# Token blocks of another size, operands in another place of the on-chip memory, and the fill of missing keys as a stage of its own

## The chip, the cores and the metric

The kernel runs on one core of one Trainium2 chip. The metric is the device time of one launch in microseconds: the median of 3 runs of the kernel before is 997.27 us (996.07 to 997.98). The core's engines work from queues of their own: TensorE (PE in the profile, with its weight loads as PEld), VectorE (DVE), ScalarE (ACT), GpSimd (POOL) and SyncE (SP), which issues most DMAs.

## The reference

Attention over chunks of 32 queries, each with 8 memory keys and up to 56 neighbouring keys, then two feed-forward stages over 3072 tokens, all in float32:

```python
for c in range(nc):                         # attention, 4 x 8 heads, 768 positions
    k_full = np.concatenate([mem_k, k[:, :, max(0, 32*c - 16):min(S, 32*c + 40)]], axis=2)
    v_full = ...                            # likewise
    a = softmax(0.125 * q_c @ k_full.T)
    out[:, :, 32*c:32*c + 32] = a @ v_full
x = out.transpose(0, 2, 1, 3).reshape(3072, 512)
x2 = ((x @ w_a) * (x @ w_b)) @ w_out        # w_a, w_b: 512 x 1536, w_out: 1536 x 512
h = x2 @ w_in                               # 512 x 1024
u = h * softmax(h)
y = ((u - mean(u)) / sqrt(var(u) + 1e-6) * g_ln) @ w_out2     # 1024 x 512
```

## The kernel before

Every product of the feed-forward stages is made of three matmuls (`mm3`, lines 376 to 378): operands are split into a high part and a rest, and high x rest, rest x high and high x high are added up in PSUM.

**Stage one** (`ab`, `gate`, `x2_step`) goes over blocks of tokens (`block_list`): 512, 256 and six times 384. In a block it goes over 12 slices f of the inner width 1536. One step f is 24 matmuls into `pab` (a and b, 12 each, over 4 slices of the model width), the gate (VectorE multiplies a and b at L393, ScalarE rounds to `gh` at L396, VectorE takes the rest `gl` at L400), and 12 matmuls into four `acc` banks (`x2_step`), which run one step later than their gate. The weights (`w`, 12 slots of 12 KB a partition) are the stationary operand; x (`xh`, `xl`) and the gate results (`gh`, `gl`) are streamed, one column a token. So a step is 36 matmuls as wide as the block. At a block's end `x2_out` writes the result to DRAM (`x2d`).

**Attention** works on quads of 4 chunks (128 tokens, 24 quads), for the block that comes next, in the slots between the matmuls of the current one: three slots a step, 36 a block. Its stages are `att_S` (fill of missing keys where a sequence begins or ends, L143 and L145, then 64 small matmuls for the scores), `att_M` (maximum), `att_X` (exponential, L174), `att_N` (normalisation, from L182), `att_T` (transposes), `att_V` (products, L219, and the copy to `xh`) and `att_L` (the rest `xl`, L242). Scores, transposed weights and products of all quads share one PSUM tile, `at`. The table in the main loop gives each stage its slot: quads are spread evenly over the slots, and for block 0 the slots are written out. The loads of q, k and v have two buffers, so a load waits for the products of the quad two before it.

**Block 0** also converts the weights of stage one (`w1_abs` to `w1_lo`: ScalarE and VectorE on 128 x 1536 pieces), and **the last block** those of stage two (`w2_*`) into slots 0 to 5.

**Stage two** goes over 24 tiles of 128 tokens: 24 matmuls of 512 columns for h (`h_mm`), softmax and normalisation, 8 transposes, 24 matmuls of 512 columns for the output (`o_mm`; the last two tiles in halves of 256). Here the converted weights are streamed and the tokens are stationary.

**Order.** In the attention at the start, block 0 and the last block the order of TensorE, VectorE and ScalarE is the program's. In the blocks between only TensorE's is; a planner orders the rest.

**Memory.** Pools lie one behind the other in the order in which they are opened: constants, `wp` (weight slots 0 to 5, 72 KB a partition), `wq` (slots 6 to 11, 72 KB), loads, attention tiles and conversion tiles (some 38 KB), then `xp` (x of two blocks, 28 KB) and `gp` (10 KB). All from `wq` on is given back after stage one, and stage two's tiles lie from the start of `wq`.

Of the kernel before, what the change touches and what calls it, by code (L numbers as in the profile page):

```python
# [8 lines left out]
F32 = mybir.dt.float32  # L9
# [9 lines left out]
P = 128  # L19
B, H, S, D = 4, 8, 768, 64  # L20
NMEM = 8
CQ = 32
CK = 64
NCH = 4
GQ = NCH * CQ
# [3 lines left out]
NG = S // GQ  # L29
NP = H // 2  # L30
# [4 lines left out]
NF2 = DFF2 // P  # L35
# [5 lines left out]
NEG = -3.0e38  # L41
# [6 lines left out]

def block_list():

    sizes = [512, 256] + [384] * 6
    out, t = [], 0
    for n in sizes:
        out.append((t, n))
        t += n
    assert t == NTOK
    return out
# [3 lines left out]
def fused_kernel(  # L61
# [9 lines left out]
    nc = tc.nc  # L71
# [3 lines left out]

    const = ctx.enter_context(tc.tile_pool(name="const", bufs=1))
    dram = ctx.enter_context(tc.tile_pool(name="dram", bufs=1, space=bass.MemoryType.DRAM))
    wp = ctx.enter_context(tc.tile_pool(name="wp", bufs=1))

    ident = const.tile([P, P], F32, name="ident")  # L80
    gln_sb = const.tile([P, NF2], F32, name="gln_sb")
    mhalf = const.tile([P, 1], F32, name="mhalf")

    x2d = [dram.tile([P, NP, n], F32, name=f"x2d{i}") for i, (_, n) in enumerate(blocks)]

    work = ExitStack()
    wq = work.enter_context(tc.tile_pool(name="wq", bufs=1))
    ld_p = work.enter_context(tc.tile_pool(name="ld", bufs=2))
# [1 line left out]
    at_p = work.enter_context(tc.tile_pool(name="atp", bufs=2))  # L90
    z_p = work.enter_context(tc.tile_pool(name="zp", bufs=2))
    sm_p = work.enter_context(tc.tile_pool(name="sm", bufs=3))
    x_p = work.enter_context(tc.tile_pool(name="xp", bufs=1))
    g_p = work.enter_context(tc.tile_pool(name="gp", bufs=2))
    ps_at = work.enter_context(tc.tile_pool(name="ps_at", bufs=1, space=PSUM))
    ps_ab = work.enter_context(tc.tile_pool(name="ps_ab", bufs=1, space=PSUM))
    ps_acc = work.enter_context(tc.tile_pool(name="ps_acc", bufs=4, space=PSUM))
# [2 lines left out]
    quads = {}  # L100
# [10 lines left out]
    def slot_tile(i, shape, dtype, name):  # L111

        return (wp if i < NS2 else wq).tile(shape, dtype, tag=f"w{i}", name=name)

    def att_load(qi, slot=None):


        n = NP * (GQ + GK) + NCH * NP * D
        if slot is None:
            t = ld_p.tile([P, n], F32, tag="qkv", name="qkv")  # L120
        else:
            t = slot_tile(slot, [P, n], F32, "qkv")
        q, k = NP * GQ, NP * (GQ + GK)
        if slot is None:
            nc.sync.dma_start(t, qkv[qi])
        else:
            nc.sync.dma_start(t[:, 0:k], qkv[qi, :, 0:k])
        quads[qi] = dict(
            q=t[:, 0:q].rearrange("d (p t) -> d p t", p=NP),
            k=t[:, q:k].rearrange("d (p t) -> d p t", p=NP),  # L130
            v=t[:, k:n].rearrange("k (c p d) -> k c p d", c=NCH, p=NP),
        )
        return lambda: nc.sync.dma_start(t[:, k:n], qkv[qi, :, k:n])

    def att_S(qi):


        st = quads[qi]
        g = qi % NG
        full = ps_at.tile([P, 2, 512], F32, tag="at", name="s")  # L140
        s = full[:, :, 0:NP * CK].rearrange("q r (p k) -> q r p k", p=NP)
        if g == 0:
            nc.vector.memset(s[0:CQ, :, :, 0:16], NEG)  # L143
        if g == NG - 1:
            nc.vector.memset(s[GQ - CQ:GQ, :, :, 56:64], NEG)  # L145
        for p in range(NP):
            for c in range(NCH):
                lo = 16 if (g == 0 and c == 0) else 0
                hi = 56 if (g == NG - 1 and c == NCH - 1) else CK
                k0 = (c // 2) * KW + (c % 2) * CQ  # L150
                for r in range(2):
                    rows = slice(64 * r, 64 * r + 64)
                    nc.tensor.matmul(
                        s[CQ * c:CQ * c + CQ, r, p, lo:hi],
                        st["q"][rows, p, CQ * c:CQ * c + CQ],
                        st["k"][rows, p, k0 + lo:k0 + hi],
                        start=True,
                        stop=True,
                    )
        st["s"] = s  # L160

    def att_M(qi):
        s = quads[qi]["s"]
# [6 lines left out]
    def att_X(qi):  # L170
        st = quads[qi]
        s = st.pop("s")
        e = a_p.tile([P, NP, 2, CK], F32, tag="E", name="E")
        nc.scalar.activation(  # L174
            out=e.rearrange("q p r k -> q r p k"), in_=s, func=AF.Exp, scale=SCALE
        )
        st["e"] = e.rearrange("q p r k -> q (p r) k")
# [80 lines left out]
    def w_range(z):  # L258

        zi = z.bitcast(I32)  # L260
        nc.vector.tensor_scalar(out=z, in0=z, scalar1=W_LO, scalar2=W_HI, op0=ALU.max, op1=ALU.min)
        nc.vector.tensor_scalar(
            out=zi, in0=zi, scalar1=3, scalar2=0x3FFFFFF8,
            op0=ALU.logical_shift_left, op1=ALU.bitwise_and,
        )
# [43 lines left out]
    def w1_range(f, part=None):  # L309
        cols = slice(0, NS * WC) if part is None else slice(part * WC, (part + 1) * WC)  # L310
        w_range(zs[f][0][:, cols])
# [235 lines left out]
    def N(i):  # L547
        att_N(i, nc.vector)
# [7 lines left out]

    w1_abs(0, 0)
    w1_range(0, 0)
    att_S(0)
    att_M(0)  # L560
    w1_abs(0, 1)
    att_X(0)
    w1_range(0, 1)
    att_S(1)
    N(0)
    w1_abs(0, 2)
# [1 line left out]
    att_M(1)  # L568
    w1_range(0, 2)
    att_X(1)  # L570
    att_S(2)
    w1_sign(0)
    w1_low(0)
# [3 lines left out]
    att_M(2)  # L577
    att_L(0)
    att_X(2)
    att_S(3)  # L580
    w1_add(0)
    w1_hi(0)
# [34 lines left out]
    for bi in range(NB):  # L617
        qs = slots_for(bi)
        nslots = 3 * NF1
        plan = {}  # L620
        if qs:
            stages = (att_S, att_M, att_X, att_N, att_T, att_V, att_L)
            per = (nslots - 6) / len(qs)
            for j, qi in enumerate(qs):
                b0 = int(j * per)
                at = [b0 + k for k in (0, 0, 0, 0, 4, 5, 5)]
                if bi == 0:

                    at = ((27, 28, 28, 29, 31, 32, 33), (30, 30, 30, 31, 33, 34, 35))[j]
                for k, fn in zip(at, stages):  # L630
                    plan.setdefault(k, []).append((fn, qi))
            att_load(qs[0])
            if bi == 0:
                att_load(qs[1])
        loaded = 1 if bi else 2
        slot = 0

        def run_slot():
            nonlocal slot, loaded
            for fn, qi in plan.get(slot, []):  # L640
                fn(qi)
                if fn is att_V and loaded < len(qs):
                    att_load(qs[loaded])
                    loaded += 1
            slot += 1

        for f in range(NF1):
            if (bi, f) == (1, 0):

                in_order.close()  # L650
                in_order.enter_context(tc.manual_schedule(engines={ENG.PE}))
            if (bi, f) == (NB - 1, 0):
                in_order.close()
                in_order.enter_context(
                    tc.manual_schedule(engines={ENG.PE, ENG.DVE, ENG.Activation})
                )

            c0, c1 = (f - 4, f - 3) if bi == NB - 1 else (-1, -1)
            n = blocks[bi][1]
            pa = ab(bi, f, 0)  # L660
            a_sb = g_p.tile([P, n], F32, tag="asb", bufs=1, name="asb", padded_shape=[P, NMAX])
            nc.scalar.copy(a_sb, pa)  # L662
            run_slot()
            pb = ab(bi, f, 1)
            if bi == 0 and f + 3 < NF1:
                w1_abs(f + 3)
            if 0 <= c1 < NS2:
                w2_abs(c1)
            gh, gl = gate(bi, a_sb, pb)
            if bi == 0 and f + 2 < NF1:  # L670
                w1_add(f + 2)
                w1_hi(f + 2)
            if 0 <= c0 < NS2:
                w2_add(c0)
                w1_hi(c0)
            gate_lo(a_sb, gh, gl)
            if bi == 0 and f + 3 < NF1:
                w1_low(f + 3)
                w1_range(f + 3)
            if bi == 0 and f + 2 < NF1:  # L680
                w1_lo(f + 2)
            if bi == 0 and f + 3 < NF1:
                w1_sign(f + 3)
            if 0 <= c1 < NS2:
                w1_low(c1)
                w_range(zs[c1][0])
            if 0 <= c0 < NS2:
                w2_lo(c0)
            if 0 <= c1 < NS2:
                w1_sign(c1)  # L690
            run_slot()
            if pend is not None:
                x2_step(*pend)
                if pend[1] == NF1 - 1:
                    x2_out(pend[0])
            pend = (bi, f, gh, gl)
            run_slot()
            if bi == 0 and f == NF1 - 1:
                x2_step(*pend)
                x2_out(0)  # L700
                pend = None
            if bi == NB - 1 and 1 <= f <= NS2:

                w2_load(f - 1)
# [117 lines left out]
```

## Time and profile before

| | |
|---|---|
| median of 3 runs | 997.27 us (996.07 to 997.98) |
| profiled execution, its time | 996.04 us |
| its span, first to last instruction | 994.3 us |
| mean granted clock of TensorE | 0.998 of full speed |
| busy: PE, DVE, ACT, POOL | 963.1, 480.0, 305.5, 38.0 us |
| attention at the start and block 0 | to 147.4 us |
| blocks 1 to 7 | 147.4 to 703.1 us |
| stage two | from 704.0 us |

Times in the rows are microseconds from the start of the span, unless they are marked ns. Matmuls are pipelined: the duration of one runs from its start to its end and overlaps the next, so what a matmul costs is the distance from start to start. A tile name like `pab<-xh,w` is what an instruction writes and reads, and L376 is a line of the kernel. What stands in brackets at a row's end is idle time of the engine before it and what ended it. The granted clock is the share of the full 2.4 GHz that TensorE was given.

### The profile page before, as it was taken

What the parts mean: (1) busy time and instruction counts of PE and PEld (TensorE: products, weight loads), DVE (VectorE), ACT (ScalarE), POOL (GpSimd) and SP (SyncE); (2) the same over time, 40 slices, a digit from 0 to 9 for tenths busy, and PEclk for the clock granted to TensorE, in tenths of its full rate; (3) what the DMA queues carried; (4) which work ended last, traced back from release to release, by engine and by line L of the source; (5) the groups of instructions that cost most, each with busy time, mean ns of one, the idle gap of its engine ahead of it and who ended that gap; (6) DMA issues with size and microseconds to landing.
All of it is one profiled execution on the core that took longest, in us unless ns stands there. A gap on an engine that the chain in (4) does not pass through costs nothing.

```text
span 994.3 us, 18094 instructions
## 1 busy us (share of the span) xinstructions
PE 963.1 (97%) x8016; PEld 878.0 (88%) x8016; DVE 480.0 (48%) x783; ACT 305.5 (31%) x464; POOL 38.0 (4%) x54
## 2 busy tenths in 40 slices
PE   4899899999999999999999999998999999999998
PEld 3688679999999999999999999998878888888887
DVE  6999933323223223322322322298575656665553
ACT  4777522222222212122222221364232332222222
POOL 0000000000000000000000000000000000000000
PEclk9999999999999999999999999999999999999999
DMA  9950032211101112111110100451211111111000
GB/s 374 423 251 1 1 117 72 97 61 57 49 32 49 49 49 80 49 48 61 68 49 31 51 1 1 162 209 33 84 43 43 44 43 53 43 43 40 25 22 33
DMA packets 27631, 75.62 MB, mean 76 GB/s; under 512 B 2016, under 2 KB 16864, under 8 KB 23584
## 3 DMA queue, kind: packets, MB, share of 16 engines
q1 hardware_dynamic: 27280, 73.67, 20.2%
q8 instruction: 63, 1.03, 0.5%
q0 software_dynamic: 272, 0.79, 0.3%
q14 instruction: 16, 0.13, 0.0%
HBM read 61.87 MB, written 12.58 MB: 75 GB/s over the span
## 4 chain that ended last, share of the span: by engine, by line
PE 84%; DVE 11%; issue 3%; DMA 1%; ACT 1%; SPq 0%; POOL 0%; DVEq 0%; ACTq 0%
PE pab L376 11%; PE pab L378 11%; PE pab L377 11%; PE acc L376 6%; PE acc L377 6%; PE acc L378 6%; PE psh L455 4%; PE pso L514 4%; PE pso L513 4%; PE pso L515 4%; PE psh L456 4%; PE psh L457 4%; PE px L219 3%; DVE z L277 3%; DVE z L269 2%
## 5 line engine op out<-in xcount | busy, mean ns | idle before, releaser
L376 PE MATMUL pab<-xh,w 128*128 128x384 f32 (+2 forms) x768 | 264.5, 344 | 3.2 <-ACT asb L662 2.2
L377 PE MATMUL pab<-xl,w 128*128 128x384 f32 (+2 forms) x768 | 259.3, 338 | 0.0
L378 PE MATMUL pab<-xh,w 128*128 128x384 f32 (+2 forms) x768 | 259.2, 337 | 0.0
L393 DVE TENSOR_TENSOR asb<-asb,pab 128x384 f32<-128x384 f32 (+2 forms) x96 | 53.1, 553 | 253.8 <-PE pab L378 253.8
L376 PEld LDWEIGHTS pab<-xh,w 128*128 128x128 f32 x768 | 144.9, 189 | 11.3 <-ACT asb L662 3.2
L377 PEld LDWEIGHTS pab<-xl,w 128*128 128x128 f32 x768 | 145.1, 189 | 4.5 <-DVE xl L242 0.2
L378 PEld LDWEIGHTS pab<-xh,w 128*128 128x128 f32 x768 | 144.9, 189 | 4.6
L377 PE MATMUL acc<-gl,w 128*128 128x384 f32 (+2 forms) x384 | 129.5, 337 | 1.9 <-DVE gl L400 1.8
L376 PE MATMUL acc<-gh,w 128*128 128x384 f32 (+2 forms) x384 | 131.2, 342 | 0.0
L378 PE MATMUL acc<-gh,w 128*128 128x384 f32 (+2 forms) x384 | 129.1, 336 | 0.0
L662 ACT COPY asb<-pab 128x384 f32<-128x384 f32 (+2 forms) x96 | 45.8, 477 | 179.9 <-PE pab L378 179.2
L396 ACT CAST gh<-asb 128x384 fp32r<-128x384 f32 (+2 forms) x96 | 49.3, 514 | 159.3 <-DVE asb L393 159.3
L514 PE MATMUL pso<-w,ll 128*128 128x512 f32 (+1 forms) x208 | 79.5, 383 | 0.6 <-DVE ll L502 0.6
L513 PE MATMUL pso<-w,lh 128*128 128x512 f32 (+1 forms) x208 | 77.9, 375 | 1.5 <-ACT lh L501 1.5
L515 PE MATMUL pso<-w,lh 128*128 128x512 f32 (+1 forms) x208 | 77.7, 374 | 0.0
L377 PEld LDWEIGHTS acc<-gl,w 128*128 128x128 f32 x384 | 72.1, 188 | 5.0 <-DVE gl L400 2.9
L455 PE MATMUL psh<-w,x2hl 128*128 128x512 f32 x192 | 75.0, 390 | 0.6 <-ACT x2hl L437 0.6
L457 PE MATMUL psh<-w,x2hl 128*128 128x512 f32 x192 | 74.9, 390 | 0.0
L456 PE MATMUL psh<-w,x2hl 128*128 128x512 f32 x192 | 74.8, 390 | 0.0
L376 PEld LDWEIGHTS acc<-gh,w 128*128 128x128 f32 x384 | 72.1, 188 | 2.9
L400 DVE TENSOR_TENSOR gl<-asb,gh 128x384 fp32r<-128x384 f32 (+2 forms) x96 | 53.4, 557 | 42.9 <-ACT gh L396 42.9
L378 PEld LDWEIGHTS acc<-gh,w 128*128 128x128 f32 x384 | 72.1, 188 | 2.2
(67 smaller groups left out, 1056.4 us busy)
## 6 DMA issues: line engine op xcount, KB each, us to landing
qkv<-qkv_dram SPq DMA_DIRECT2D x20, 1152.0 KB, 5.6
raw<-w1d_dram SPq DMA_DIRECT2D x11, 1536.0 KB, 24.8
out_dram<-ot SPq DMA_DIRECT2D x22, 256.0 KB, 2.0
x2r<-x2d SPq DMA_DIRECT2D x21, 256.0 KB, 3.1
x2d<-x2s SPq DMA_DIRECT2D x12, 384.0 KB, 2.5
raw<-win_dram SPq DMA_DIRECT2D x8, 512.0 KB, 5.4
raw<-wout_dram SPq DMA_DIRECT2D x8, 512.0 KB, 5.0
qkv<-qkv_dram SPq DMA_DIRECT2D x4, 640.0 KB, 9.1
```

Source lines behind the costliest of these rows:

```text
L376: nc.tensor.matmul(ps, wl, xh, start=first, stop=False)
L377: nc.tensor.matmul(ps, wh, xl, start=False, stop=False)
L378: nc.tensor.matmul(ps, wh, xh, start=False, stop=last)
L393: nc.vector.tensor_tensor(out=a_sb, in0=a_sb, in1=pb, op=ALU.mult)
L396: nc.scalar.copy(gh, a_sb)
L400: nc.vector.tensor_tensor(out=gl, in0=a_sb, in1=gh.bitcast(F32), op=ALU.subtract)
L455: nc.tensor.matmul(ps[:, hf], a, w[:, 1], start=(k == 0), stop=False)
L456: nc.tensor.matmul(ps[:, hf], b, w[:, 0], start=False, stop=False)
L457: nc.tensor.matmul(ps[:, hf], a, w[:, 0], start=False, stop=(k == NP - 1))
L513: nc.tensor.matmul(po, s["lh"][:, f], wl, start=(f == 0), stop=False)
L514: nc.tensor.matmul(po, s["ll"][:, f], wh, start=False, stop=False)
L515: nc.tensor.matmul(po, s["lh"][:, f], wh, start=False, stop=(f == NF2 - 1))
```

## The change

The block sizes become 512, 256, 512, 384, 512, 384, 512: seven blocks instead of eight. The pools `xp` and `gp` are opened directly behind the constants, ahead of `wp`, and are no longer given back before stage two; two small constants are padded, so that `xp` begins 3072 bytes into a partition (2176 bytes of it lie ahead of the kernel's own constants). The fill of missing keys leaves `att_S` and becomes the stage `att_P`, with a slot of its own: in the middle blocks the slot of `att_S`, in block 0 slot 29 for the second quad, ahead of the first quad's normalisation there (the list of slot 29 is reversed), while `att_T` and `att_V` of block 0 go one slot later.

```diff
-    sizes = [512, 256] + [384] * 6
+    sizes = [512, 256, 512, 384, 512, 384, 512]
...
+    ident = const.tile([P, P], F32, name="ident")
+
+    gln_sb = const.tile([P, NF2], F32, name="gln_sb", padded_shape=[P, 64])
+    mhalf = const.tile([P, 1], F32, name="mhalf", padded_shape=[P, 32])
+
+    x2d = [dram.tile([P, NP, n], F32, name=f"x2d{i}") for i, (_, n) in enumerate(blocks)]
+
+
+    x_p = ctx.enter_context(tc.tile_pool(name="xp", bufs=1))
+    g_p = ctx.enter_context(tc.tile_pool(name="gp", bufs=2))
     wp = ctx.enter_context(tc.tile_pool(name="wp", bufs=1))
...
-    x_p = work.enter_context(tc.tile_pool(name="xp", bufs=1))
-    g_p = work.enter_context(tc.tile_pool(name="gp", bufs=2))
...
+    def att_P(qi):
+        full = ps_at.tile([P, 2, 512], F32, tag="at", name="s")
+        s = full[:, :, 0:NP * CK].rearrange("q r (p k) -> q r p k", p=NP)
+        if qi % NG == 0:
+            nc.vector.memset(s[0:CQ, :, :, 0:16], NEG)
+        if qi % NG == NG - 1:
+            nc.vector.memset(s[GQ - CQ:GQ, :, :, 56:64], NEG)
+        quads[qi]["s"] = s
+
     def att_S(qi):
...
-        full = ps_at.tile([P, 2, 512], F32, tag="at", name="s")
-        s = full[:, :, 0:NP * CK].rearrange("q r (p k) -> q r p k", p=NP)
-        if g == 0:
-            nc.vector.memset(s[0:CQ, :, :, 0:16], NEG)
-        if g == NG - 1:
-            nc.vector.memset(s[GQ - CQ:GQ, :, :, 56:64], NEG)
+        s = st["s"]
...
+    att_P(0)
     att_S(0)
...
-            stages = (att_S, att_M, att_X, att_N, att_T, att_V, att_L)
+            stages = (att_P, att_S, att_M, att_X, att_N, att_T, att_V, att_L)
             per = (nslots - 6) / len(qs)
             for j, qi in enumerate(qs):
                 b0 = int(j * per)
-                at = [b0 + k for k in (0, 0, 0, 0, 4, 5, 5)]
+                at = [b0 + k for k in (0, 0, 0, 0, 0, 4, 5, 5)]
                 if bi == 0:
 
-                    at = ((27, 28, 28, 29, 31, 32, 33), (30, 30, 30, 31, 33, 34, 35))[j]
+                    at = ((27, 27, 28, 28, 29, 32, 33, 33), (29, 30, 30, 30, 31, 34, 35, 35))[j]
                 for k, fn in zip(at, stages):
                     plan.setdefault(k, []).append((fn, qi))
+            if bi == 0:
+
+                plan[29].reverse()
```

`att_P` also stands ahead of each of the other three `att_S` of the attention at the start.

## Rows read from the trace of the kernel before

**Rows 1.** The page: busy us (share) and count; granted clock in 40 slices, tenths.

```profile
PE 963.1 (97%) x8016; PEld 878.0 (88%) x8016; DVE 480.0 (48%) x783; ACT 305.5 (31%) x464; POOL 38.0 (4%) x54
...
PEclk9999999999999999999999999999999999999999
```

**Rows 2.** Timeline of TensorE, block 0: start us, us, instruction; six steps lie between.

```profile
58.38 0.40 PE L376 MATMUL pab<-xh,w 128*128 128x512 f32 x1
...
108.78 0.40 PE L376 MATMUL pab<-xh,w 128*128 128x512 f32 x1
```

**Rows 3.** Timeline of TensorE, block 3 (384 columns), two steps apart.

```profile
352.16 0.33 PE L376 MATMUL pab<-xh,w 128*128 128x384 f32 x1
...
364.64 0.33 PE L376 MATMUL pab<-xh,w 128*128 128x384 f32 x1
```

**Rows 4.** Timeline of TensorE, block 1 (256 columns), one step apart.

```profile
196.90 0.28 PE L376 MATMUL pab<-xh,w 128*128 128x256 f32 x1
...
201.14 0.28 PE L376 MATMUL pab<-xh,w 128*128 128x256 f32 x1
```

**Rows 5.** Timeline of TensorE, stage two: 44 matmuls apart, then 22 (256 columns).

```profile
819.92 0.39 PE L513 MATMUL pso<-w,lh 128*128 128x512 f32 x1
...
829.90 0.39 PE L515 MATMUL pso<-w,lh 128*128 128x512 f32 x1
...
987.91 0.28 PE L514 MATMUL pso<-w,ll 128*128 128x256 f32 x1
...
990.55 0.28 PE L515 MATMUL pso<-w,lh 128*128 128x256 f32 x1
```

**Rows 6.** Windows, block 3 and the last: us, busy of PE to POOL, clock, DMA, GB/s.

```profile
287.92:370.88 82.96, 82.96 (x830) 80.97 (x830) 23.16 (x44) 17.87 (x35) 3.13 (x3) 1.00 0.15 54
...
619.77:703.06 83.29, 79.24 (x445) 76.84 (x444) 54.40 (x65) 37.60 (x46) 2.29 (x3) 1.00 0.36 121
```

**Rows 7.** Timeline of VectorE, last block: four gates in turn.

```profile
656.97 0.55 DVE L393 TENSOR_TENSOR asb<-asb,pab 128x384 f32<-128x384 f32 x1
...
664.77 0.55 DVE L393 TENSOR_TENSOR asb<-asb,pab 128x384 f32<-128x384 f32 x1
...
673.10 0.55 DVE L393 TENSOR_TENSOR asb<-asb,pab 128x384 f32<-128x384 f32 x1
...
682.21 0.55 DVE L393 TENSOR_TENSOR asb<-asb,pab 128x384 f32<-128x384 f32 x1
```

**Rows 8.** Timeline of TensorE, last block: the starts of two steps in turn.

```profile
671.01 0.45 PE L376 MATMUL pab<-xh,w 128*128 128x384 f32 x1 [0.80 <-ACT asb L662]
...
680.13 0.45 PE L376 MATMUL pab<-xh,w 128*128 128x384 f32 x1 [0.78 <-ACT asb L662]
```

**Rows 9.** Timeline of all engines, block 0, up to the scores of quad 5.

```profile
122.78 0.60 ACT L174 ACTIVATE E<-s 128x512 f32<-128x512 f32 x1 [3.22 <-DVE s L166]
...
123.41 0.69 DVE L182 TENSOR_REDUCE sm<-E 128x8 f32<-128x512 f32 x1 [0.72 <-ACT E L174]
...
124.63 0.11 DVE L145 MEMSET s<- 32x64 f32 x1
...
124.84 0.89 PE L153 MATMUL s<-qkv 64*32 64x64 f32 x64 [3.71 <-ACT asb L662]
```

**Rows 10.** Timeline of VectorE, block 0: the gates of the steps f = 1 and 9.

```profile
51.02 0.68 DVE L393 TENSOR_TENSOR asb<-asb,pab 128x512 f32<-128x512 f32 x1
...
115.64 0.69 DVE L393 TENSOR_TENSOR asb<-asb,pab 128x512 f32<-128x512 f32 x1
```

**Rows 11.** Windows, the end of block 0: columns as in rows 6.

```profile
121.00:130.00 9.00, 5.29 (x77) 4.14 (x77) 4.22 (x9) 1.67 (x3) 1.04 (x1) 0.81 0.01 2
```

**Rows 12.** Timeline of all engines, block 1: products of its first quad, and their rest.

```profile
156.54 1.14 PE L219 MATMUL px<-AT,qkv 64*64 64x32 f32 x64
...
158.37 0.69 DVE L242 TENSOR_TENSOR xl<-px,xh 128x512 fp32r<-128x512 f32 x1 [2.74 <-ACT xh L237]
```

**Rows 13.** The page, DMA issues: count, KB each, median us from issue to landing.

```profile
qkv<-qkv_dram SPq DMA_DIRECT2D x20, 1152.0 KB, 5.6
```

More of the change, by code (lines that the diff above doesn't have):

```diff
@@ L77, in fused_kernel @@
     dram = ctx.enter_context(tc.tile_pool(name="dram", bufs=1, space=bass.MemoryType.DRAM))
+    ident = const.tile([P, P], F32, name="ident")
[4 more added lines that the diff above has]
+    g_p = ctx.enter_context(tc.tile_pool(name="gp", bufs=2))
     wp = ctx.enter_context(tc.tile_pool(name="wp", bufs=1))
[L80 to L84, printed above, removed]
     work = ExitStack()
@@ L159, in att_S @@
                     )
-        st["s"] = s
     def att_M(qi):
@@ L563, in fused_kernel @@
     w1_range(0, 1)
+    att_P(1)
     att_S(1)
@@ L570, in fused_kernel @@
     att_X(1)
+    att_P(2)
     att_S(2)
@@ L579, in fused_kernel @@
     att_X(2)
+    att_P(3)
     att_S(3)
```

## The prediction

> **What bounds the kernel now.** I read the page first: TensorE is busy for 97% of the span [rows 1], so the question is what one matmul costs. Busy time cannot say it, because matmuls overlap; the timeline can, from start to start over whole steps with no attention work in them. In block 0 six steps of 36 matmuls of 512 columns run from 58.38 to 108.78 us: 233.3 ns each [rows 2]. At 384 columns two steps run from 352.16 to 364.64: 173.3 ns [rows 3]. At 256 columns one step runs from 196.90 to 201.14: 117.8 ns [rows 4]. Stage two has 512 columns as well, and there 44 matmuls run from 819.92 to 829.90: 226.8 ns; its 256-column ones take 120.0 ns (22 from 987.91 to 990.55) [rows 5].
>
> At 2.4 GHz, the clock granted in all these stretches, 512, 384 and 256 columns take 213.3, 160.0 and 106.7 ns. What stands above that is 13.5 ns (512) and 13.3 ns (256) in stage two, and 20.0, 13.3 and 11.1 ns (512, 384, 256) in stage one. So only the 512-column matmul of stage one is dear. Its operands differ from stage two's in place: by the pools' sizes x, gh and gl lie behind 144 KB of weights and 38 KB of working tiles, from about 182 KB of a partition on, while stage two streams weights that lie in the lowest 75 KB. The weights' own place doesn't show: the steps of rows 2 take theirs from slots up to 75 KB apart, at one rate.
>
> Then the stages where TensorE waits. The windows give 82.96 us for a block of 384, busy throughout, and for the last block, which has no attention work beside it, 83.29 with 79.24 busy [rows 6]. In the last block VectorE converts stage two's weights, and it is the bound: its gates (L393) start 7.8, 8.3 and 9.1 us apart [rows 7], and TensorE's step beginning at 671.01 lasts 9.12 us where 36 x 173.3 ns = 6.24 are work [rows 8]. Last, the end of block 0: TensorE stops for 3.7 us before the scores of quad 5 (124.84) [rows 9]; the row names a copy of ScalarE (L662), but the scores also need the fill (L145), and that ends last, at 124.74.
>
> **The change part by part.** All sums are against the profiled execution, 996.04 us with a span of 994.27; the median of the runs is 997.27, 1.2 higher.
>
> *Block sizes.* Each block has 12 steps of 36 matmuls, 432. Behind block 0, before: 432 x (0.1178 + 6 x 0.1733) = 500.2 us. After, at the old price of 512 columns: 432 x (0.1178 + 3 x 0.2333 + 2 x 0.1733) = 503.0, so +2.9 us. Wider blocks alone lose.
>
> *x and the gate results in the lowest memory.* The trace has no stage-one matmul with its operands there. Nearest rows: stage two's 226.8 at 512 and 120.0 at 256, and its 13.3 to 13.5 ns over the columns give 173.3 at 384 [rows 5]. Bounds for 512: 213.3 (columns alone) and 233.3 (no effect). I take 226.8, the row with the operand low: 432 x (0.1200 + 3 x 0.2268 + 2 x 0.1733) = 495.5, so -4.7 us together with the sizes.
>
> The Trainium skill speaks against this: its page "SBUF — State Buffer", section "Who interferes with whom", gives TensorE separate read ports for the moving operand and for weights, and says that TensorE never waits on anyone. It names no cost of an operand's place. By it the 512 columns would stay at 233.3 and the sum of this part at +2.9. Against it stands that the same 512 columns take two prices here [rows 2, 5].
>
> *Block 0.* Its matmuls get cheaper too, but mostly for nothing. VectorE's gates are (115.64 - 51.02) / 8 = 8.08 us apart with work between them throughout, and TensorE's steps 8.40 [rows 2, 10]. At 226.8 a step is 8.16, and TensorE only arrives earlier at the scores of quad 5, whose start VectorE's chain sets. Only the 72 matmuls behind that point count: 72 x 6.5 ns = -0.5 us.
>
> *The fill as a stage.* The fill of quad 5 (L145, 0.11 us) is queued on VectorE behind the normalisation of quad 4 (from L182 on). It needs only the bank that the exponential (L174) frees at 122.78 + 0.60 = 123.38. In the new order it runs at 123.41 instead of 124.63, so the scores start at about 123.6 instead of 124.84: -1.2 us [rows 9]. The fill issues no DMA and passes no queue but VectorE's; behind it the normalisation is 0.11 us later, and its reader, the transpose, goes one slot later anyway (12 matmuls, 2.8 us), so that costs nothing. What is late next is still this chain; the wait stays about as long, as TensorE comes earlier. I leave the fall of the clock that follows it (mean granted clock 0.81 in 121 to 130 us [rows 11]) as it is. The mean stands for 9 x 0.19 / 0.5 = 3.4 us at 1.2 GHz; without them 1.7 us more would go. In other blocks the fill stays in its slot: nothing.
>
> *Last block.* TensorE's step becomes 36 x 226.8 ns = 8.16 us. VectorE's gates come to two instructions of 0.68 instead of 0.55 us (rows 7 beside rows 10), so their distances grow by 0.27 to 8.1, 8.6 and 9.4. Against 8.16 the lag adds up to 0.4 + 1.2 = 1.7 us. The gate's result is read 36 matmuls later and its bank refilled 24 later (5.4 us), so a lag of 1.7 reaches nobody. Before, the step of 6.24 was behind by 1.6, 2.1 and 2.9 in turn. The loss before is 83.29 less 444 x 0.1733 (76.95) = 6.3 us; all of it goes: -6.3. If the cover were gone, the 1.7 would return.
>
> *Four quads during blocks 1, 3 and 5.* Behind block 0 there are 18 quads before and after. In block 1 slots are 12 x 0.12 = 1.4 us and quads now 7 or 8 slots apart instead of 10. The next scores come two slots (2.8 us) behind the products (L219) that hold the bank. From the end of the products (156.54 + 1.14 = 157.68) to the end of L242 (159.06) took 1.4 us [rows 12]: hidden, 0 to 1 us if VectorE is busy; I take +0.3. The loads of q, k and v wait for the products two quads earlier, 10 slots or 14 us ahead, and land in 5.6 us [rows 13]: hidden.
>
> *Sum.* -4.7 - 0.5 - 1.2 - 6.3 + 0.3 = -12.4 us: 983.6 for the profiled execution. With the 1.2 by which this execution lies under the median: 984.8.
>
> **The rivals.**
>
> *No effect of place (0.18).* 512 stays at 233.3: +2.9 - 1.2 - 6.3 + 0.3 = -4.3, 991.7 us (993.0 from the median). The last block still pays, as its step is 8.40. For it: 384 and 256 columns are not dear in high memory. Against: the two prices of 512. This is also where the skill's rule above would end.
>
> *The 13.3 ns go too (0.09).* The tiles are padded to even starts; if what stands above the columns comes from how rows begin, all widths fall to column time: 432 x (0.1067 + 3 x 0.2133 + 2 x 0.16) = 460.8, so -39.4, with block 0, the fill and the last block -8.9: about 948, and with 1152 matmuls of stage two at 13.4 ns (-15.5) 932. For it: the excess varies with something besides the width. Against: stage two has 13.3 at two widths and in every slot; no row is lower in steady running. The Trainium skill ("TensorE: Matmul & The Clock Gate", "Back-to-back issue gap") gives 512 columns some 216 ns warm; no long run of fp32r matmuls here reaches that.
>
> *Slower: the new places are dear ones (0.13).* If the extra 6.5 ns come from how the moving rows lie to the weights, and not from height, the layout can put them on all widths and, as the weights move up by the 38 KB that x and the gates take, on stage two: 512 at 233.3, 384 at 179.8, 256 at 126.5. Then 2592 + 72 matmuls of stage one and 1152 of stage two cost 6.5 ns more than in my sum: +24.8 - 12.4 = +12.4, 1008.4 us. It decides from 3.3 ns on. For it: the weights leave the lowest memory, where they had the good rate. Against: they run at one rate over 70 KB of slots.
>
> **How the numbers follow.** Forecast 0.60, no effect of place 0.18, all overhead gone 0.09, dear places 0.13. The forecast's own range is 981 to 989: a point each for the 256-column price, for the clock and for block 1's crowding, and up to 4 us if only part of the 6.5 ns goes. The range 973 to 995 takes in the rival without effect and the start of the other two. A measurement of this kernel can tell 0.2%, 2 us. Faster holds the first three cases less their tails and a little of the last, 0.84; no change 0.05; slower 0.11.
>
> **What would show it.** Timeline: steps of 512 columns in blocks 2, 4 and 6 at 8.16 us (8.40: no effect of place; 7.7: all overhead gone), of 384 at 6.24, stage two at 226.8. Windows of the last block: TensorE busy throughout. Block 0: the fill directly behind L174 and the scores at about 123.6. Wrong if stage two slows or 384 columns rise above 173.3.

## The result, and the profile after

The changed kernel takes 984.24 us in the median (983.15 to 985.29, 4 runs) against 996.67 us before (four runs; the 997.27 above is the median of the first three): ratio 0.9878, interval 0.9866 to 0.9889. The forecast was 984.8 us. The profiled execution took 983.15 us, its span 981.4, so 12.9 us less than the profiled one before.

Three rows of the page after: busy time by engine, TensorE's granted clock in tenths, and the chain of waits by engine.

```profile
PE 954.7 (97%) x7584; PEld 823.1 (84%) x7584; DVE 478.0 (49%) x757; ACT 301.7 (31%) x438; POOL 37.8 (4%) x54
...
PEclk9999999999999999999999999999999999999999
...
PE 87%; DVE 9%; issue 2%; ACT 1%; DMA 0%; POOL 0%; ACTq 0%; DVEq 0%
```

There are 432 matmuls fewer, one block's worth, and TensorE is still the bound. The price of a matmul answers to [rows 2 to 5]. The timeline of TensorE in the kernel after (start us, duration, instruction): two starts that lie two steps of 512 columns apart in block 4, then two that lie one step of 384 apart in block 3, then two that lie one step of 256 apart in block 1.

```profile
479.30 0.39 PE L381 MATMUL pab<-xh,w 128*128 128x512 f32 x1
...
495.62 0.39 PE L381 MATMUL pab<-xh,w 128*128 128x512 f32 x1
...
385.54 0.33 PE L381 MATMUL pab<-xh,w 128*128 128x384 f32 x1
...
391.77 0.34 PE L381 MATMUL pab<-xh,w 128*128 128x384 f32 x1
...
197.77 0.28 PE L381 MATMUL pab<-xh,w 128*128 128x256 f32 x1
...
202.09 0.28 PE L381 MATMUL pab<-xh,w 128*128 128x256 f32 x1
```

16.32 / 72 = 226.7 ns at 512 columns, where [rows 2] gave 233.3. 6.23 / 36 = 173.1 ns at 384, as [rows 3]. 4.32 / 36 = 120.0 ns at 256, where [rows 4] gave 117.8. Stage two takes 290.3 us in both kernels.

The windows of the kernel after answer to [rows 6, 11]: the end of block 0, block 1 and the last block (us, busy time of PE, PEld, DVE, ACT and POOL, clock, DMA share, GB/s).

```profile
121.00:130.00 9.00, 7.46 (x87) 6.04 (x88) 4.33 (x10) 2.29 (x4) 1.04 (x1) 0.81 0.01 2
144.90:206.41 61.51, 61.23 (x950) 59.44 (x948) 22.73 (x49) 16.43 (x37) 4.17 (x4) 1.00 0.30 107
...
590.33:690.21 99.88, 99.88 (x445) 83.01 (x444) 57.92 (x65) 40.41 (x46) 2.30 (x3) 1.00 0.29 100
```

TensorE is busy throughout the last block: the 4 us in which [rows 6] show it idle are gone. The clock still falls at the end of block 0 (0.81), as in [rows 11].

The timeline around the scores of quad 5 in the kernel after answers to [rows 9]. L143 is now the fill and L187 the normalisation.

```profile
121.69 0.60 ACT L179 ACTIVATE E<-s 128x512 f32<-128x512 f32 x1 [3.22 <-DVE s L171]
122.37 0.11 DVE L143 MEMSET s<- 32x64 f32 x1 [0.78 <-ACT E L179]
122.39 0.62 DVE L187 TENSOR_REDUCE sm<-E 128x8 f32<-128x512 f32 x1
...
122.54 0.95 PE L159 MATMUL s<-qkv 64*32 64x64 f32 x64 [4.62 <-DVE s L143]
```

The fill now stands ahead of the normalisation, 0.08 us behind the end of the exponential (121.69 + 0.60), and the row of the scores names it as what they waited for. TensorE waits longer than before, 4.62 us against 3.71, because it comes earlier.

### The profile page after: what moved, and what is told of

Its sections match the earlier page's. It is cut to its first block, busy times and chain, and to the rows that moved or that the text cites. A ratio compares the mean times of both kernels' runs of the same rounds, so it can differ in the third digit from the quotient of the medians.

```text
span 981.4 us, 17140 instructions
## 1 busy us (share of the span) xinstructions
PE 954.7 (97%) x7584; PEld 823.1 (84%) x7584; DVE 478.0 (49%) x757; ACT 301.7 (31%) x438; POOL 37.8 (4%) x54
## 4 chain that ended last, share of the span: by engine, by line
PE 87%; DVE 9%; issue 2%; ACT 1%; DMA 0%; POOL 0%; ACTq 0%; DVEq 0%
PE pab L381 12%; PE pab L383 11%; PE pab L382 11%; PE acc L381 6%; PE acc L383 6%; PE acc L382 6%; PE pso L519 4%; PE pso L518 4%; PE psh L461 4%; PE pso L520 4%; PE psh L462 4%; PE psh L460 4%; PE px L224 2%; PE pst L503 2%; DVE z L282 2%
## 5 line engine op out<-in xcount | busy, mean ns | idle before, releaser
L381 PE MATMUL pab<-xh,w 128*128 128x512 f32 (+2 forms) x672 | 247.0, 368 | 0.5 <-ACT xh L242 0.5
L383 PE MATMUL pab<-xh,w 128*128 128x512 f32 (+2 forms) x672 | 242.6, 361 | 0.0
L382 PE MATMUL pab<-xl,w 128*128 128x512 f32 (+2 forms) x672 | 242.5, 361 | 0.0
L398 DVE TENSOR_TENSOR asb<-asb,pab 128x512 f32<-128x512 f32 (+2 forms) x84 | 51.3, 610 | 227.5 <-PE pab L383 222.8
L381 PEld LDWEIGHTS pab<-xh,w 128*128 128x128 f32 x672 | 127.6, 190 | 17.4 <-ACT xh L242 0.6
L383 PEld LDWEIGHTS pab<-xh,w 128*128 128x128 f32 x672 | 127.4, 190 | 15.5
L381 PE MATMUL acc<-gh,w 128*128 128x512 f32 (+2 forms) x336 | 122.5, 365 | 0.0
L383 PE MATMUL acc<-gh,w 128*128 128x512 f32 (+2 forms) x336 | 120.7, 359 | 0.0
L382 PE MATMUL acc<-gl,w 128*128 128x512 f32 (+2 forms) x336 | 120.5, 359 | 0.0
L674 ACT COPY asb<-pab 128x512 f32<-128x512 f32 (+2 forms) x84 | 43.9, 523 | 171.7 <-PE pab L383 170.9
L401 ACT CAST gh<-asb 128x512 fp32r<-128x512 f32 (+2 forms) x84 | 47.0, 560 | 149.5 <-DVE asb L398 149.4
L405 DVE TENSOR_TENSOR gl<-asb,gh 128x512 fp32r<-128x512 f32 (+2 forms) x84 | 52.6, 627 | 37.7 <-ACT gh L401 37.7
L381 PEld LDWEIGHTS acc<-gh,w 128*128 128x128 f32 x336 | 63.3, 188 | 8.2
L383 PEld LDWEIGHTS acc<-gh,w 128*128 128x128 f32 x336 | 63.2, 188 | 7.6
```

The source lines that it names most:

```text
L381: nc.tensor.matmul(ps, wl, xh, start=first, stop=False)
L382: nc.tensor.matmul(ps, wh, xl, start=False, stop=False)
L383: nc.tensor.matmul(ps, wh, xh, start=False, stop=last)
L398: nc.vector.tensor_tensor(out=a_sb, in0=a_sb, in1=pb, op=ALU.mult)
L401: nc.scalar.copy(gh, a_sb)
L405: nc.vector.tensor_tensor(out=gl, in0=a_sb, in1=gh.bitcast(F32), op=ALU.subtract)
```

## The experiments

The theory after the result: the 512-column matmul is cheaper because of where x and the gate results lie, and the last block because a wider step covers VectorE. What "where" means was open. Height: rows far up in the memory are streamed slower. Offset: it matters how the streamed rows lie to the weights, modulo some small unit. In the kernel before x begins 186,656 bytes behind the start of the weights, 32 more than a multiple of 256. Stage two's operands and those of the changed kernel lie a multiple of 1024 apart. An offset that is a multiple of 256 bytes is called even below. So the change moved both at once.

**x and the gate results back at the top.**

```diff
-    gln_sb = const.tile([P, NF2], F32, name="gln_sb", padded_shape=[P, 64])
-    mhalf = const.tile([P, 1], F32, name="mhalf", padded_shape=[P, 32])
+    gln_sb = const.tile([P, NF2], F32, name="gln_sb")
+    mhalf = const.tile([P, 1], F32, name="mhalf")
...
-    x_p = ctx.enter_context(tc.tile_pool(name="xp", bufs=1))
-    g_p = ctx.enter_context(tc.tile_pool(name="gp", bufs=2))
...
     sm_p = work.enter_context(tc.tile_pool(name="sm", bufs=3))
+    x_p = work.enter_context(tc.tile_pool(name="xp", bufs=1))
+    g_p = work.enter_context(tc.tile_pool(name="gp", bufs=2))
```

> The changed kernel with x and the gate results back behind all other pools and without the padding, so at exactly the bytes of a partition where the kernel before had them; block sizes and the fill's stage stay changed. Both theories (height: rows high in the memory are streamed slower; offset: the price goes by how the streamed rows lie to the stationary weights, modulo some small unit) expect the old prices: 512 columns at 233.3 ns, 256 at 117.8. That is 432 x 3 x 6.6 ns = 8.5 us more in blocks 2, 4 and 6, 0.5 more at the end of block 0, 1.0 less in block 1: about 8 us over the changed kernel, 992 us, ratio to before 0.995. If place is not the cause at all, 984.

991.41 us, ratio 0.995 (0.9935 to 0.9965). The place is worth 7.2 us of the 12.4; seven blocks at the old prices win only 5.1 us, the fill's 1.2 among them.

**At the top, but at an even offset.** Against the run before it, this is added:

```diff
     sm_p = work.enter_context(tc.tile_pool(name="sm", bufs=3))
+    pad_p = work.enter_context(tc.tile_pool(name="pad", bufs=1))
+    pad_p.tile([P, 184], F32, name="pad")                         # 736 bytes
     x_p = work.enter_context(tc.tile_pool(name="xp", bufs=1))
```

> As the run before it (x and gate results at the top, from 190144 bytes on), but with 736 bytes of padding ahead of them, so that x lies to the weights at a multiple of 1024 bytes (190144 - 2752 = 183 x 1024), as stage two's operands do, instead of 288 bytes off. Height theory: still 233.3 ns for 512 columns, 992 us. Offset theory: 226.7 ns for 512 and 120 for 256, 984 us as the changed kernel.

984.38 us, ratio 0.988 (0.9863 to 0.9896): all of it, at the top of the memory.

**Low, but at the old offset.**

```diff
-    mhalf = const.tile([P, 1], F32, name="mhalf", padded_shape=[P, 32])
+    mhalf = const.tile([P, 1], F32, name="mhalf", padded_shape=[P, 24])
...
     g_p = ctx.enter_context(tc.tile_pool(name="gp", bufs=2))
+    pad_p = ctx.enter_context(tc.tile_pool(name="pad", bufs=1))
+    pad_p.tile([P, 184], F32, name="pad")
     wp = ctx.enter_context(tc.tile_pool(name="wp", bufs=1))
```

> The changed kernel with x and the gate results in the lowest memory, but 32 bytes lower (3040) and with 736 bytes of padding between them and the weights (42688), so that both have the offsets modulo 1024 of the kernel before (992 and 704, 288 apart). Height theory: 226.7 ns for 512 columns, 984 us. Offset theory: 233.3 for 512 and 117.8 for 256 columns, 992 us, and stage two unchanged at 226.7, as its operands keep a multiple of 1024 between them.

990.95 us, ratio 0.9945 (0.993 to 0.996): nothing of it, in the lowest memory. One step of 512 columns in block 4, first in the kernel with x at the top and even:

```profile
488.30 0.39 PE L383 MATMUL pab<-xh,w 128*128 128x512 f32 x1
...
496.46 0.39 PE L383 MATMUL pab<-xh,w 128*128 128x512 f32 x1
```

and then in the one with x low and at the old offset:

```profile
491.39 0.39 PE L383 MATMUL pab<-xh,w 128*128 128x512 f32 x1
...
499.79 0.39 PE L383 MATMUL pab<-xh,w 128*128 128x512 f32 x1
```

8.16 us against 8.40, 226.7 ns against 233.3. The height theory falls, and with it what I took the low place for.

**The price by itself.** Its core, for each group:

```python
for i in range(24):
    s0 = stationary // 4 + 128 * (i % 4)
    nc.tensor.matmul(ps[:, 0:n], big[:, s0:s0 + 128], big[:, streamed // 4:streamed // 4 + n],
                     start=(i == 0), stop=(i == 23))
```

> Measures the disputed cost by itself and computes nothing of the reference: 52 groups of 24 matmuls back to back, each with its own weight load (four stationary pieces in turn), over one large tile, with the streamed rows at chosen offsets (0 to 992 bytes modulo 1024) to the weights, at 512, 384 and 256 columns, low (16 KB), at 192 KB and at 208 KB. Height theory: 226.7 ns at 512 columns in the low groups whatever the offset, and 233.3 in the high ones. Offset theory: the same price low and high, 226.7 at offset 0 and 233.3 at 288, and other offsets show the unit; 384 and 256 columns at 173.3 and 117.8 at 288, and 173.3 and 120.0 at 0. Should some offset give less than 13 ns over the columns (213.3, 160.0, 106.7), a faster layout exists.

Parts of four groups in its timeline, 512 columns each (start, time from the first start to the last end, instruction, number of matmuls in the part; one execution): offsets 256 and 288 with the streamed rows at 16 KB, and 0 and 288 with them at 192 KB.

```profile
66.75 4.47 PE L108 MATMUL ps<-big 128*128 128x512 f32 x19
...
72.69 4.13 PE L108 MATMUL ps<-big 128*128 128x512 f32 x17
...
196.82 4.24 PE L108 MATMUL ps<-big 128*128 128x512 f32 x18
...
202.06 4.59 PE L108 MATMUL ps<-big 128*128 128x512 f32 x19
```

A matmul's own 0.39 taken off and shared out over the distances: 4.08 / 18 = 226.7, 3.74 / 16 = 233.8, 3.85 / 17 = 226.5 and 4.20 / 18 = 233.3 ns. The means of the last 20 distances of a group, in ns, by the offset in bytes:

```
512 columns   0 (192 KB): 226.7   256: 227.2   512: 226.7   768: 226.7
              32: 233.3    64: 228.8    96: 233.9   128: 233.3   160: 234.3   192: 233.3   224: 233.3
              288: 233.3   320: 228.8   352: 233.9   384: 233.3   448: 233.3   640, 896, 960, 992: 233.3
384 columns   0, 32, 64, 256, 288, 512, 768: 173.3   128: 176.0   992: 173.9
256 columns   0: 119.3   256: 119.8   512, 768: 120.0   32, 64, 288: 117.8   128: 118.7   992: 118.2
both operands shifted by 32, 512 columns: offset 0: 226.7   offset 288: 233.3
streamed rows at 208 KB, 512 columns: offset 0: 227.8   offset 288: 233.3
```

The first group of all, offset 0 at 16 KB, is left out: its first matmuls lie 426 ns apart, twice the 213.3 of their columns, as at 1.2 GHz.

At 512 columns the pattern repeats every 256 bytes. Only the offset between the two operands counts there: neither the height nor a shift of both by 32 bytes changes the price by more than about 1 ns. Multiples of 256 bytes are the cheapest of all tried and save 6.6 ns; at 384 the offset hardly matters, and at 256 columns the even offset is the dearer one, by some 2 ns. No offset tried reaches column time, so the rival in which all overhead goes has no layout among them.

**The old block sizes, all else new.**

```diff
-    sizes = [512, 256, 512, 384, 512, 384, 512]
+    sizes = [512, 256] + [384] * 6
```

> The changed kernel with the old block sizes (512, 256 and six times 384) and everything else new. Prediction with the offset theory: 384 columns cost the same either way, so of the gain only the fill (-1.2), the end of block 0 (-0.5) and, against them, 256 columns at 120.0 instead of 117.8 (+1.0) are left: about 996 us, ratio to before 0.999, and the last block's wait of 6.3 us is back. Rival: the place is worth something by itself, in any width, and then 990 or less.

995.62 us, ratio 0.9988 (0.9979 to 0.9998). By itself the new place is worth next to nothing, as the table says for 384 columns. Its last block, in the windows, waits as before: 83.24 us with 79.22 busy.

```profile
618.72:701.96 83.24, 79.22 (x445) 76.67 (x444) 54.41 (x65) 37.86 (x46) 2.29 (x3) 1.00 0.35 121
```

Sizes and fill win 5.1 us, place and fill 1.3, all three 12.4: the difference comes from the 512-column matmuls, which are many only with the new sizes and cheap only with the new offset.

**Less for VectorE in the last block**, in the kernel before and in the changed one:

```diff
             if 0 <= c1 < NS2:
                 w1_low(c1)
-                w_range(zs[c1][0])
...
-            if 0 <= c1 < NS2:
-                w1_sign(c1)
```

> The kernel before without three of VectorE's instructions a piece in the last block (the clamp, the shift and the sign of the conversion of stage two's weights; 3.7 us of some 7.8 a step). Prediction's step: the last block waits for VectorE alone, so its 6.3 us go: 990.3 us, ratio to before 0.9937. Rival: TensorE there waits for the loads of these weights or for ScalarE, and the time stays at 996.5.

990.18 us, ratio 0.9938 (0.9923 to 0.9953): VectorE alone held TensorE there. In its profiled execution TensorE is busy for all of the last block's 78.45 us.

> The changed kernel without the same three instructions. Prediction's step: with steps of 8.16 us VectorE's lag reaches nobody, so nothing is left to gain there: 984.2 us, as the changed kernel. Rival: a rest of the wait is left in the last block, and 1 to 2 us go.

984.47 us against 984.24, ratio 0.9877 (0.9862 to 0.9892): the wider step covers all of it. The last block takes 100.78 us in both profiled executions.

**The fill back behind the normalisation.**

```diff
-    at = ((27, 27, 28, 28, 29, 32, 33, 33), (29, 30, 30, 30, 31, 34, 35, 35))[j]
+    at = ((27, 27, 28, 28, 29, 31, 32, 33), (30, 30, 30, 30, 31, 33, 34, 35))[j]
...
-                plan[29].reverse()
```

> The changed kernel with the fill of quad 5 back in the slot of its scores and block 0's table as in the kernel before (transposes and products one slot earlier again). Prediction's step: the fill is again queued behind the normalisation of quad 4, so the scores of quad 5 start 1.2 us later and the whole takes about 1.2 us more than the changed kernel, 985.4 us against 984.2. Rival: the bank or another engine holds the scores, the fill's place is worth nothing, 984.2.

985.54 us (984.60 to 985.68), ratio 0.9887 (0.987 to 0.9903): 1.3 us more, though the intervals of the two ratios overlap, and the clock differs too: from 121 to 130 us its mean is 0.62 in this profiled execution and 0.81 in the changed kernel's. The changed kernel with less for VectorE has the same block 0 as the changed kernel and shows 0.62 as well; its block 0 took 112.83 us (33.90 to 146.73), against 114.57 here (32.58 to 147.15). So at a like clock the fill back, with the transposes and products one slot earlier, costs 1.7 us in these two executions. The timeline shows the order of before again:

```profile
122.30 0.69 DVE L187 TENSOR_REDUCE sm<-E 128x8 f32<-128x512 f32 x1 [0.72 <-ACT E L179]
...
123.52 0.11 DVE L143 MEMSET s<- 32x64 f32 x1
...
123.73 1.14 PE L159 MATMUL s<-qkv 64*32 64x64 f32 x64 [5.82 <-ACT asb L671]
```

Counted from the start of block 0 (32.58 here, 32.59 in the changed kernel), the scores start 91.15 us later instead of 89.95: 1.2 us of it. The row names ScalarE's copy (L671) again, which had ended at 122.75; the fill ends at 123.63.

**A version that uses the wait.** VectorE sets when these scores can start, so TensorE can do other work first:

```diff
-    at = ((27, 27, 28, 28, 29, 32, 33, 33), (29, 30, 30, 30, 31, 34, 35, 35))[j]
+    at = ((27, 27, 28, 28, 29, 32, 33, 33), (29, 31, 31, 31, 32, 34, 35, 35))[j]
```

> The changed kernel with the scores, maximum, exponential and normalisation of quad 5 one slot later in block 0 (31 instead of 30), so behind the second half of the step's matmuls into pab. Theory of the prediction (VectorE's chain, up to the fill that ends some 90 us after block 0 begins, sets these scores' start, and TensorE comes too early): TensorE does 12 matmuls (2.7 us) while it would wait, its wait falls from 5.0 to some 2.3 us, and 2.7 us go; if the clock no longer falls to 1.2 GHz behind it, another 1.7: 981.5 to 979.8 us, ratio to before 0.984. Rival: the scores, or the transposes of quad 4 that share their bank, only become late by the same time, and it stays at 984.2.

980.49 us, ratio 0.9834 (0.982 to 0.9847): faster than both. In its timeline and windows the wait is 1.87 us, and the clock stays at 2.4 GHz.

```profile
123.38 0.11 DVE L143 MEMSET s<- 32x64 f32 x1 [0.78 <-ACT E L179]
...
123.55 0.84 PE L159 MATMUL s<-qkv 64*32 64x64 f32 x64 [1.87 <-DVE s L143]
...
127.83 0.60 ACT L179 ACTIVATE E<-s 128x512 f32<-128x512 f32 x1 [2.15 <-DVE s L171]
...
128.58 0.63 PE L200 MATMUL pt<-ident,E 128*128 128x128 f32 x4 [1.24 <-ACT E L179]
```

```profile
121.00:130.00 9.00, 5.89 (x89) 4.36 (x88) 6.20 (x14) 2.88 (x5) 1.30 (x2) 1.00 0.01 2
```

The gain is 3.75 us in the medians. In the two profiled executions block 0 falls by 2.9 us (from 112.31 to 109.43), less than the 4.4 of wait and clock together: the transposes of quad 4 (L200) now wait 1.24 us for the exponential of quad 5 (L179), which holds their bank. That the medians gain more is probably the clock again: its mean over an execution is 0.996 or 0.997 in three of the changed kernel's four, 0.998 in the profiled one, and 1.000 in all five here.

## Why the prediction was right, and where its reason was not

- *Price of a matmul.* Forecast 226.8, 173.3 and 120.0 ns; measured 226.7, 173.1 and 120.0. From the start of block 1 to the first matmul of stage two the time fell from 556.53 (147.42 to 703.95) to 546.21 us (144.90 to 691.11): -10.3, against -4.7 - 6.3 + 0.3 = -10.7.
- *The reason for it.* Here the step "x and the gate results in the lowest memory" failed: I took stage two's price because its streamed operand lies low. The price came out right because the change also made the offset even, as stage two's is; height plays no part. That was luck. The offset stood in the prediction only inside the slower rival. Its mechanism is the true one, but the layout fell on the good side and no width became 6.5 ns dearer (256 columns became 2.2 ns dearer). What the prediction held against that rival, one rate over 70 KB of weight slots, could not count: the slots are 12 KB apart, a multiple of 256 bytes, so the streamed rows had the same offset to all of them, modulo 256. With x just as low but at the old offset, the forecast would have missed by 6 us (990.95).
- *The rule of the Trainium skill* ("SBUF — State Buffer", "Who interferes with whom": TensorE has separate read ports for the two operands and waits on no one). It holds as to other engines in what is seen here: the same price stands beside a busy VectorE in block 0 (75.07 of 75.41 us, first row; six steps there from 50.10 to 99.06 us are 226.7 ns a matmul) and a mostly idle one in block 4 (2.76 of 16.32, second row). It doesn't tell of the 6.6 ns that TensorE's own two operands cost each other, and a time worked out by it would have come to the rival without effect.

```profile
32.59:108.00 75.41, 75.41 (x322) 62.14 (x323) 75.07 (x66) 53.66 (x47) 0.00 (x0) 1.00 0.42 177
479.30:495.62 16.32, 16.32 (x74) 13.52 (x73) 2.76 (x4) 2.41 (x4) 0.00 (x0) 1.00 0.10 43
```

- *Last block.* Forecast -6.3 with nothing left. From its start to stage two it took 84.18 us before, 7.2 more than its 444 matmuls, and takes 100.78 after, where 432 x 0.2267 + 12 x 0.1733 = 100.0 is matmuls: -6.4, with 0.8 left. Both experiments with less work for VectorE agree, and the 0.8 is not VectorE's, as it stays without the three instructions.
- *The fill.* Forecast -1.2; 124.84 - 33.63 = 91.21 us from the start of block 0 before and 122.54 - 32.59 = 89.95 after: -1.26.
- *The rest of block 0.* Forecast -0.5; from these scores to block 1 22.58 us became 22.36, -0.2. That TensorE's earlier arrival in block 0 would win nothing was right: the wait only grew.
- *Four quads in block 1.* 57.96 us became 61.51. Up to the start of block 2 there are 420 matmuls (block 1's last 12 run behind it), so 420 x 2.2 ns = 0.9 is the price of 256 columns and 2.6 the extra quad, where each of the three before took (57.96 - 420 x 0.1178) / 3 = 2.8: no crowding there. Worked out in this way for all 18 quads behind block 0, what is left beside the blocks' matmuls grew from 49.2 to 50.1 us. So the term of +0.3 measured +0.9.
- Of the 12.9 us between the two profiled executions, 1.0 belongs to none of this: block 0 started at 32.59 instead of 33.63 us. It starts at 33.76 in the kernel with x at the top and even, which has the same start; the medians differ by 12.4.

## What to carry to other kernels

Measure matmuls from start to start, by width and by place: two prices for one width are a lead, and here they were worth 7 us of 997. Where each matmul has a weight load of its own, as here, lay streamed rows and weights a multiple of 256 bytes apart when rows are 512 columns wide: with it the wider blocks and the fill won 12.4 us, without it 5.1. A guess at the reason (low memory) can give the right number and still send the next layout astray. Where an engine waits for a chain that it doesn't feed, look for its own work that can go ahead, as one slot did for 3.75 us.

## What the runs showed of the hardware that was not expected

- A matmul of 512 columns with its own weight load costs 226.7 ns when streamed rows and weights lie a multiple of 256 bytes apart, and mostly 233.3 at the other offsets tried (228.8 at 64 modulo 256). The prices at the offsets 0 and 288 are the same to about 1 ns with streamed rows at 16, 192 and 208 KB. Why the engine does so isn't shown.
- 384 columns have a second steady price with operands in the same place. In the kernel before with less work in the last block, a step there lasts 6.36 us instead of 6.24, 176.7 ns a matmul, in the whole block and in the last two steps of the block ahead of it:

```profile
677.41 0.34 PE L376 MATMUL pab<-xh,w 128*128 128x384 f32 x1
...
683.77 0.34 PE L376 MATMUL pab<-xh,w 128*128 128x384 f32 x1
```

What starts it was not tried. 12 x 0.12 = 1.4 us would about account for that execution's 991.38 us beside the median of 990.18.
- The clock fell to 1.2 GHz behind waits of 2.51 us (x back at the top), 3.71 (before), 4.62 (after) and 5.82 (the fill back), and not behind one of 1.87. From 121 to 130 us the mean granted clock is 0.81 behind the first three. It is 0.62 behind the wait of 5.82 (first row), so the half clock lasted about twice as long; but it is 0.62 also behind a wait of 4.19, in the changed kernel with less for VectorE (second row). The length of the wait alone doesn't tell how long the half clock lasts:

```profile
121.00:130.00 9.00, 6.27 (x77) 5.00 (x78) 3.14 (x7) 1.67 (x3) 1.04 (x1) 0.62 0.01 2
...
121.00:130.00 9.00, 6.15 (x78) 5.01 (x79) 4.44 (x10) 1.67 (x3) 1.04 (x1) 0.62 0.01 2
```
